# The attention loop of one core issued by whole tiles instead of half tiles, with eight filler products at the start

## The chip, the cores and the metric

The kernel runs on one core of a Trainium2 chip. A core has five instruction streams that run beside each other and wait for one another through semaphores: TensorE (PE, products and transposes; its weight loads are shown as PEld), VectorE (DVE), ScalarE (ACT), GpSimd (POOL) and SyncE (SP), which here only starts DMA transfers. Each stream keeps its own order: an instruction that waits holds up all that stand behind it on its engine. The metric is the device time of one execution in microseconds (us), as the median of several runs.

## The reference

Attention over 2 batches, 8 heads, 768 positions and head size 64, with a band of 96 local keys and 8 global ones, feeds a mixture of 4 experts and then a gated layer:

```python
scores = scale * np.matmul(q, k.transpose(0, 1, 3, 2))
...
scores = np.where(keep, scores + bias, -1000000000.0)
a = np.exp(scores - np.max(scores, axis=-1, keepdims=True))
a = a / (np.sum(a, axis=-1, keepdims=True) + 1e-09)
x = np.matmul(a, v)
...
out += p[:, e:e + 1] * (np.maximum(x @ w1[e], 0.0) @ w2[e])
...
y = ((out @ w1) * (out @ w2) @ w3) @ w_out
```

All is float32. The products behind the attention split each operand into a high and a low part and make three products of one.

## The kernel before

The change touches one function, `banded_attention`, which fills the first 79 us. It works on 12 tiles of 128 queries (6 for each batch). A tile sees 232 keys: 8 global ones, 96 before the tile and its own 128; the first tile of each batch has only its own 128. These two come first in the order of the tiles. The 8 heads of a tile are done in two **steps** of 4 heads, written (tile, 0) and (tile, 1); tiles are counted here in the order in which they are done, so that (1,1) is the second half of the second tile. There are 24 steps.

What a step needs, in the order of its data:

- **S**: 8 score products on PE (L246) into two banks of PSUM, the memory that PE writes and from which DVE and ACT read (tiles `sp`, 4 in turn).
- 4 reductions on DVE (L257), each of which adds the bias of a head and finds its row maximum, then 4 exponentials on ACT (L264), which write `pt` and the row sums. DVE and ACT hand over through the buffers `t`, of which there are 3.
- the inverse of the sums: POOL adds 1e-9 (L230), DVE takes the reciprocal (L232).
- the normalisation of `pt`: heads 0 to 2 on POOL (L304), head 3 on DVE (L308).
- **T**: 8 transposes on PE (L280) into two banks (`tp`, 2 in turn), which I call its half 0 and half 1 (two heads each); DVE copies half 0 (L292) and ACT half 1 (L290) to `ptT`.
- **V**: 16 value products on PE (L322 and L323; only 8, at L325, for the first tile of a batch) into one bank (`op`, 2 in turn).
- the split of the result: ACT writes the high part `xh` from `op` (L391), DVE subtracts it from `op` and writes the low part `xl` (L397).

The engines follow the order in which the code is written (`manual_schedule`). PE goes round by steps: S of step s, T of step s-2, V of step s-3. Steps 11 to 22 also carry one piece each of the split of the experts' first weights: ACT writes the high part (L50) and POOL the low part (L51). At the very start PE runs 11 products on zeros (`keep_warm(WARM)`, L175), and 4, 4 and 2 more behind the scores of steps 0, 1 and 2. At the end, three products of the experts (`up_ahead`, L56 to L58) are put between the last steps. From the first of them the rest of the program is unchanged.

Of the kernel before, what the change touches and what calls it, by code (L numbers as in the profile page):

```python
# [8 lines left out]
F32 = mybir.dt.float32  # L9
# [4 lines left out]
ALU = mybir.AluOpType  # L14
AF = mybir.ActivationFunctionType
# [3 lines left out]
P = 128  # L19
B, H, S, D = 2, 8, 768, 64  # L20
NQ = S // P
# [96 lines left out]
def banded_attention(tc, g, x_hi, x_lo, slots, experts):  # L118
    nc = tc.nc
    with ExitStack() as ctx:  # L120
# [15 lines left out]

        order = [b * NQ for b in range(B)] + [u for u in range(B * NQ) if u % NQ]

        steps = [(u, gr) for u in order for gr in range(2)]

        def place(u):

            return u + 1 if u < NQ else u - NQ
# [80 lines left out]
        raws = []  # L224

        def inverse_sums(u, gr, part):
            hs = slice(4 * gr, 4 * gr + 4)
# [3 lines left out]
            else:  # L231
                nc.vector.reciprocal(r, r)  # L232

        def scores(u, gr, before):
# [16 lines left out]
            sums = st[u]["sums"]  # L251
            pt = two.tile([P, 4, WIN], F32, name="pt", bufs=3)
            for hh in range(4):
                h = 4 * gr + hh
                t = three_.tile([P, WIN], F32, name="t", bufs=3)
                bb = bias[:, h] if i else bias0[:, h]
                nc.vector.tensor_tensor_reduce(  # L257
                    out=t[:, 0:w], in0=sp[hh % 2][:, hh // 2, 0:w], in1=bb, scale=-SCALE,
                    scalar=3.0e38, op0=ALU.add, op1=ALU.min, accum_out=g.negmax[:, u * H + h : u * H + h + 1],
                )  # L260

                if before and hh in (0, 2):
                    inverse_sums(*before, hh // 2)
                nc.scalar.activation(  # L264
                    pt[:, hh, 0:w], t[:, 0:w], AF.Exp, bias=g.negmax[:, u * H + h : u * H + h + 1],
                    scale=-1.0, accum_out=sums[:, h : h + 1],
                )
            st[u][gr] = pt

        def transposes(u, gr):  # L270
            i = u % NQ
            nj = 2 if i else 1
            pt = st[u][gr]
            tps = []
            for half in range(2):
                tp = ps_t.tile([P, 2, 2, P], F32, name="tp")
                for hh in range(2):
                    for j in range(nj):
# [5 lines left out]
        def copies(u, gr):  # L284
            nj = 2 if u % NQ else 1
            res = []
            for half, tp in enumerate(st[u][gr]):
                sb = two.tile([P, 2, 2, P], F32, name="ptT", bufs=4)
                if half:
                    nc.scalar.copy(sb[:, :, 0:nj], tp[:, :, 0:nj])  # L290
                else:
                    nc.vector.tensor_copy(sb[:, :, 0:nj], tp[:, :, 0:nj])  # L292
                res.append(sb)
            st[u][gr] = res

        def normalize(u, gr):
# [13 lines left out]
        def values(u, gr):  # L310

            i = u % NQ
            va, vo = values_of[u]
            o = ps_o.tile([P, 2, 2 * P], F32, name="op")
            st[u].setdefault("o", []).append(o)
            for hh in range(4):
                h, ab = 4 * gr + hh, hh % 2
                sb = st[u][gr][hh // 2]
                os_ = o[ab * D : (ab + 1) * D, hh // 2, 0:P]
                vs = slice(h * D, (h + 1) * D)  # L320
                if i:
                    nc.tensor.matmul(os_, va[:, vs], sb[0 : LW + GW, ab, 0], start=True, stop=False)  # L322
# [2 lines left out]
                    nc.tensor.matmul(os_, vo[:, vs], sb[:, ab, 0], start=True, stop=True)  # L325

        def outputs(u, gr):
            return st[u]["o"][gr][:, :, 0:P], x_hi, x_lo, u, slice(2 * gr, 2 * gr + 2)


        ns = len(steps)
        for s in range(ns + 3):
            n = s - W_STEP
            if 0 <= n <= 12 and n % 4 == 0:
                raws.append(two.tile([P, F], F32, name="wr"))
                nc.sync.dma_start(raws[-1], g.w_moe[0, n // 4])
            if 4 <= s < ns:
                split_x_hi(nc, *outputs(*steps[s - 4]))
            if s < ns:
                u, gr = steps[s]  # L340
                if gr == 0 and s // 2 + 2 < len(order):
                    fetch(order[s // 2 + 2])
                if gr == 1 and s // 2 + 1 < len(order):
                    fetch_v(order[s // 2 + 1])
                scores(u, gr, steps[s - 1] if s else None)
                if s == 0:
                    first_bias(1)
                    later_distances()
                if s in (2, 3):
                    later_bias(s - 2)  # L350
                if s < len(FILL) and FILL[s]:
                    keep_warm(FILL[s])
            if 0 <= s - 2 < ns:
                transposes(*steps[s - 2])
                copies(*steps[s - 2])
            if s == ns:
                inverse_sums(*steps[-1], 0)
                inverse_sums(*steps[-1], 1)
            if 0 <= s - 1 < ns:
                normalize(*steps[s - 1])  # L360
            if 4 <= s < ns:
                split_x_lo(nc, *outputs(*steps[s - 4]))
            if s >= 3:
                values(*steps[s - 3])
            if s >= ns:
                for step in steps[s - 4 : s - 2] if s == ns else (steps[s - 3],):
                    split_x_hi(nc, *outputs(*step))
                for step in steps[s - 4 : s - 2] if s == ns else (steps[s - 3],):
                    split_x_lo(nc, *outputs(*step))
                experts.up_ahead(ps_s)  # L370
            if 2 <= n <= 13:
                f, part = divmod(n - 2, 4)
                ps = slice(part * (F // 4), (part + 1) * (F // 4))
                hi, lo = slots[f]
                split(nc, hi[:, ps], lo[:, ps], raws[f][:, ps], nc.gpsimd)
            if s == ns + 1:
                split(nc, *slots[3], raws[3])


def put_x(nc, g, pool, xn, x_hi, x_lo, u):  # L380
# [865 lines left out]
```

## Time and profile before

| what | value |
|---|---|
| median of 3 runs | 832.16 us (832.11 to 832.34) |
| the profiled execution's own time | 833.32 us |
| its span, first to last instruction | 831.5 us |
| PE busy in the span | 820.7 us, 99% |
| DVE, ACT, POOL busy | 62%, 34%, 37% |
| attention loop | from the start to 79.07 us |

The span is what the trace covers; the execution's own time is longer by what lies around it (1.8 us). Busy shares are means over stages that differ: in the attention loop DVE and ACT are busy nearly all the time, behind it hardly. PE is pipelined, so the distance from the start of one group to the start of the next says more than the duration shown.

### The profile page before, as it was taken

Reading aid. Unit: us, or ns where it says so; the run is one execution under the profiler, and the core shown is the slowest. Engines: PE = TensorE matmul, PEld = TensorE weight load, DVE = VectorE, ACT = ScalarE, POOL = GpSimd, SP = SyncE. Lnnn points to the kernel's source line nnn. Section 1 sums busy time; section 2 is a strip of 40 time slices with the busy share of each in tenths; the row PEclk is TensorE's granted clock in tenths of the full one; section 3 lists DMA queues with packets and bytes.
Section 4 is the critical chain, followed back from the end, with each engine's and each line's share of the span. In section 5 each row is a group of like instructions: output and inputs, shape, how many; then the busy total and the mean of one; then the engine's idle time right before and its main releaser. Section 6 shows DMA issues by size and latency. Waiting matters only on the chain.

```text
span 831.5 us, 11122 instructions
## 1 busy us (share of the span) xinstructions
PE 820.7 (99%) x4006; PEld 668.9 (80%) x4006; DVE 514.9 (62%) x961; ACT 286.5 (34%) x609; POOL 307.7 (37%) x317
## 2 busy tenths in 40 slices
PE   8999999999999999999999999999999999999996
PEld 4777888888888888888888888888788888888875
DVE  7997356557755556787738563665633743887840
ACT  6997321224311213334323321332443332333210
POOL 3686023535356464550344341422380003333300
PEclk9999999999999999999999999999999999999999
DMA  6662233547553556643101101120522210201011
GB/s 205 215 190 64 78 123 106 165 159 238 160 165 114 166 165 202 222 157 103 62 26 52 39 25 64 43 73 27 192 99 91 86 51 26 101 26 51 2 51 55
DMA packets 38295, 88.14 MB, mean 106 GB/s; under 512 B 3722, under 2 KB 10170, under 8 KB 38230
## 3 DMA queue, kind: packets, MB, share of 16 engines
q1 hardware_dynamic: 38230, 87.33, 32.6%
q8 instruction: 34, 0.56, 0.3%
q14 instruction: 31, 0.25, 0.1%
HBM read 73.66 MB, written 13.66 MB: 105 GB/s over the span
## 4 chain that ended last, share of the span: by engine, by line
PE 91%; POOL 3%; ACT 2%; DVE 1%; issue 1%; POOLq 0%; ACTq 0%; DVEq 0%
PE z L56 18%; PE z L58 18%; PE z L57 18%; PE o L58 11%; PE o L56 11%; PE o L57 11%; POOL pt L304 2%; ACT pt L264 1%; POOL sl L51 1%; PE tp L175 1%; PE sp L246 1%; PE tp L280 1%; PE op L322 1%; PE sp L56 0%; PE op L323 0%
## 5 line engine op out<-in xcount | busy, mean ns | idle before, releaser
L58 PE MATMUL z<-xh,sl 128*128 128x512 f32 x428 | 166.6, 389 | 0.0
L56 PE MATMUL z<-xh,sh 128*128 128x512 f32 x428 | 166.5, 389 | 0.0
L57 PE MATMUL z<-xl,sh 128*128 128x512 f32 x428 | 166.5, 389 | 0.0
L494 POOL TENSOR_TENSOR cr<-cr,cb 128x512 f32<-128x512 f32 x40 | 51.6, 1289 | 126.9 <-issue 119.1
L51 POOL TENSOR_TENSOR sl<-wr,sh 128x256 fp32r<-128x256 f32 (+1 forms) x44 | 40.9, 944 | 150.1 <-ACT sh L50 149.5
L58 PEld LDWEIGHTS z<-xh,sl 128*128 128x128 f32 x428 | 80.4, 188 | 17.2 <-DVE sl L51 0.2
L57 PEld LDWEIGHTS z<-xl,sh 128*128 128x128 f32 x428 | 80.4, 188 | 16.8
L56 PEld LDWEIGHTS z<-xh,sh 128*128 128x128 f32 x428 | 80.3, 188 | 16.3
L51 DVE TENSOR_TENSOR sl<-wr,sh 128x1024 fp32r<-128x1024 f32 (+1 forms) x57 | 70.5, 1243 | 23.1 <-ACT sh L50 22.4
L50 ACT CAST sh<-wr 128x1024 fp32r<-128x1024 f32 (+2 forms) x101 | 75.5, 767 | 21.2 <-PE z L57 10.3
L746 POOL TENSOR_TENSOR acc<-acc,t 128x512 f32<-128x512 f32 x36 | 49.3, 1404 | 84.5 <-DVE t L745 84.5
L479 POOL TENSOR_SCALAR ca<-ca 128x512 f32<-128x512 f32 x40 | 61.9, 1548 | 35.3 <-ACT ca L477 35.3
L645 DVE TENSOR_TENSOR t<-t,z 128x512 f32<-128x512 f32 x56 | 37.5, 680 | 32.0 <-PE z L58 27.7
L56 PE MATMUL z<-sh,sh 128*128 128x512 f32 x128 | 49.9, 390 | 0.7 <-DVE t L745 0.7
L58 PE MATMUL z<-sh,sl 128*128 128x512 f32 x128 | 49.8, 389 | 0.0
L57 PE MATMUL z<-sl,sh 128*128 128x512 f32 x128 | 49.8, 389 | 0.0
L264 ACT ACTIVATE pt<-t,negmax 128x232 f32<-128x232 f32 (+1 forms) x96 | 44.3, 462 | 8.7 <-DVE negmax L257 7.6
L304 POOL TENSOR_TENSOR pt<-pt,r 128x232 f32<-128x232 f32 (+1 forms) x72 | 38.0, 555 | 15.5 <-DVE r L232 15.5
L257 DVE CUSTOM_DVE_ANT_0 t<-sp,bias 128x232 f32<-128x232 f32 (+1 forms) x96 | 32.5, 372 | 3.9 <-PE sp L246 3.0
L51 POOL TENSOR_TENSOR sl<-t,sh 128x256 fp32r<-128x256 f32 (+1 forms) x24 | 23.0, 973 | 31.2 <-ACT sh L50 31.0
L56 PE MATMUL o<-h0h,sh 128*128 128x512 f32 x84 | 32.8, 390 | 0.0
L57 PE MATMUL o<-h0l,sh 128*128 128x512 f32 x84 | 32.7, 389 | 0.0
(252 smaller groups left out, 1737.0 us busy)
## 6 DMA issues: line engine op xcount, KB each, us to landing
wr<-in_w_moe_dram SPq DMA_DIRECT2D x44, 512.0 KB
raw<-in_w3t_dram SPq DMA_DIRECT2D x16, 512.0 KB
raw<-in_w_ab_dram SPq DMA_DIRECT2D x16, 512.0 KB
wr<-wab_d SPq DMA_DIRECT2D x16, 512.0 KB
raw<-in_w_out_dram SPq DMA_DIRECT2D x8, 512.0 KB
w3t_d<-cr SPq DMA_DIRECT2D x16, 256.0 KB
wab_d<-cr SPq DMA_DIRECT2D x16, 256.0 KB
wr<-w3t_d SPq DMA_DIRECT2D x8, 512.0 KB
```

Of the source, the lines that this page charges most:

```text
L50: nc.scalar.copy(hi, src)
L51: (lo_engine or nc.vector).tensor_tensor(lo, src, hi.bitcast(F32), op=ALU.subtract)
L56: nc.tensor.matmul(out, wh, xh, start=start, stop=False)
L57: nc.tensor.matmul(out, wh, xl, start=False, stop=False)
L58: nc.tensor.matmul(out, wl, xh, start=False, stop=stop)
L257: nc.vector.tensor_tensor_reduce(out=t[:, 0:w], in0=sp[hh % 2][:, hh // 2, 0:w], in1=bb, scale=-SCALE, scalar=3.0e38, op0=ALU.add, op1=ALU ...
L264: nc.scalar.activation(pt[:, hh, 0:w], t[:, 0:w], AF.Exp, bias=g.negmax[:, u * H + h : u * H + h + 1], scale=-1.0, accum_out=sums[:, h : h ...
L304: nc.gpsimd.tensor_tensor(pt[:, hh, 0:w], pt[:, hh, 0:w], r[:, hh : hh + 1].to_broadcast([P, w]), op=ALU.mult)
L479: nc.gpsimd.tensor_scalar(a, a, 2.0**-15, None, op0=ALU.max)
L494: nc.gpsimd.tensor_tensor(rest, rest, top.bitcast(F32), op=ALU.add)
L645: add = lambda o, a, b: nc.vector.tensor_tensor(o, a, b, op=ALU.add)
L746: nc.gpsimd.tensor_tensor(acc[c][:, d], acc[c][:, d], t, op=ALU.add)
```

## The change

The loop no longer goes round by steps but by tiles. In tile m, with `one_back` and `two_back` for the tiles before, PE now issues S(m,0), S(m,1), T(one_back,0), V(two_back,1), V(one_back,0), T(one_back,1). The other engines' code is written in an order to go with it. Besides that:

- `WARM` is 8 instead of 11.
- V of two steps that follow each other on PE now fills two halves of one bank: `op` is a tile of 4x128 and each step takes 2x128 of it. There are still 2 such banks, and 8 banks in all.
- POOL normalises all 4 heads in the first tiles (m up to 5); from m = 6 on (`shared`) head 3 is DVE's as before.
- `pt` has 4 buffers instead of 3.
- The low parts of two steps (`low(gone)`) follow the copy of T(one_back,0), half 0, on DVE; the high parts (`high(gone)`) end the tile on ACT.

In the changed file the scores are at L244, the reductions at L259, the reciprocal at L230, the transposes at L275, the copies at L282, DVE's normalisation at L297, the values at L314, L315 and L317, and `xl` at L454.

```diff
-WARM = 11
+WARM = 8
...
-            o = ps_o.tile([P, 2, 2 * P], F32, name="op")
-            st[u].setdefault("o", []).append(o)
+            if not banks or len(banks[-1][1]) == 2:
+                banks.append((ps_o.tile([P, 4, P], F32, name="op"), []))
+            o = banks[-1][0][:, 2 * len(banks[-1][1]) :][:, 0:2]
+            banks[-1][1].append((u, gr))
+            st[u]["o", gr] = o
...
-                if hh < 3:
+                if hh < 3 or not shared:
...
-        for s in range(ns + 3):
...
-                scores(u, gr, steps[s - 1] if s else None)
...
-                transposes(*steps[s - 2])
-                copies(*steps[s - 2])
...
-                normalize(*steps[s - 1])
...
-                split_x_lo(nc, *outputs(*steps[s - 4]))
-            if s >= 3:
-                values(*steps[s - 3])
...
+        for m, u in enumerate(order):
+            one_back, two_back = (order[m - k] if m >= k else None for k in (1, 2))
+            shared = 11 <= 2 * m <= 22
...
+            scores(u, 0)
...
+            scores(u, 1)
...
+            if m >= 2:
+                for half in range(2):
+                    copy(two_back, 1, half)
+            rest = piece(2 * m)
+            if m:
+                inverse_sums(one_back, 1, 0)
+            weights(u, 0, 0)
+            if m:
+                inverse_sums(one_back, 1, 1)
+            weights(u, 0, 1)
+            if m:
+                transposes(one_back, 0)
+                copy(one_back, 0, 1)
+            weights(u, 0, 2)
+            weights(u, 0, 3)
...
+            if m:
+                copy(one_back, 0, 0)
+                low(gone)
+                normalize(one_back, 1, shared)
+            rest()
...
+            inverse_sums(u, 0, 0)
+            weights(u, 1, 0)
+            weights(u, 1, 1)
+            inverse_sums(u, 0, 1)
+            weights(u, 1, 2)
+            weights(u, 1, 3)
...
+            normalize(u, 0, shared)
+            rest()
+            gone = [(two_back, 1)] if m >= 2 else []
+            gone += [(one_back, 0)] if m else []
+            for step in gone:
+                values(*step)
+            if m:
+                transposes(one_back, 1)
+            high(gone)
...
+        values(prior, 1)
+        experts.up_ahead(ps_s)
+        values(last, 0)
+        transposes(last, 1)
...
+        experts.up_ahead(ps_s)
+        values(last, 1)
...
+        experts.up_ahead(ps_s)
```

Here a function `weights` is one head's reduction and exponential, `copy` one of the two copies behind a T, `inverse_sums(..., 0)` POOL's part of the inverse and `inverse_sums(..., 1)` DVE's; `rest` is a weight piece's low part on POOL.

The order of the instructions on two engines shows the move. The number behind a name is the program's number of that buffer's use (an `op` with the same number is the same bank in the same use), and what an instruction waits for is given as the engine or DMA queue whose semaphore it watches.

PE before, one step in the middle of the loop (`sp` scores, `tp` transposes, `op` values):

```order
L246 MATMUL sp_925<-keys_96,qr_638 128x232
...
L280 MATMUL tp_946<-ident_63,pt_818 128x128 [waits DVE_49,Pool_49]
...
L280 MATMUL tp_951<-ident_63,pt_818 128x128 [waits Activation_49,Pool_49]
...
L322 MATMUL op_965<-ptT_900,va_695 64x128 [waits DMAHW7_49,DVE_49]
L323 MATMUL op_965<-ptT_900,vo_693 64x128 [waits DMAHW6_49]
...
L322 MATMUL op_965<-ptT_902,va_695 64x128
...
L246 MATMUL sp_980<-keys_96,qr_749 128x232 [waits DMAHW1_49,DMAHW0_49]
```

One S, one T and one V alternate, and each V has a bank of its own number.

PE after, tile m = 7 from the end of its scores on:

```order
L244 MATMUL sp_867<-keys_96,qr_627 128x232 [waits DVE_49]
...
L275 MATMUL tp_887<-ident_63,pt_754 128x128 [waits DVE_49,Pool_49]
...
L275 MATMUL tp_892<-ident_63,pt_754 128x128 [waits Activation_49,Pool_49]
...
L314 MATMUL op_830<-ptT_874,va_524 64x128 [waits DVE_49]
...
L314 MATMUL op_830<-ptT_876,va_524 64x128
...
L314 MATMUL op_942<-ptT_905,va_632 64x128 [waits DMAHW7_49]
...
L314 MATMUL op_942<-ptT_897,va_632 64x128 [waits Activation_49]
...
L275 MATMUL tp_951<-ident_63,pt_761 128x128 [waits PE_49,Pool_49]
```

The first V (`op_830`, the second half of a bank whose first half the tile before has filled) stands right behind T(one_back,0) and waits for DVE; the second V (`op_942`, a new bank) reads `ptT_905`, which DVE writes, and has no wait for DVE of its own.

DVE before, around one copy (`xl` is the low part, `r` the sums):

```order
L257 ISA t_943,negmax_69<-sp_926,bias_97 128x232 [waits Activation_49]
...
L292 COPY ptT_956<-tp_946 128x512 [waits PE_49]
L308 TENSOR_SCALAR pt_875<-pt_875,r_874 128x232 [waits DVE_49]
L397 TENSOR_TENSOR xl1_74<-op_909,xh1_71 128x2x128
L257 ISA t_989,negmax_69<-sp_980,bias_97 128x232 [waits PE_49,Activation_49]
```

The low part there reads `op_909`, while PE is at `op_965`, another bank.

DVE after, in tile m = 7, from the copy of T(two_back,1) to the normalisation:

```order
L282 COPY ptT_874<-tp_839 128x512 [waits PE_49]
L259 ISA t_880,negmax_69<-sp_858,bias_97 128x232 [waits PE_49,Activation_49]
...
L230 RECIPROCAL r_753<-r_753 128x4 [waits Pool_49]
L259 ISA t_884,negmax_69<-sp_859,bias_97 128x232 [waits PE_49,Activation_49]
...
L282 COPY ptT_905<-tp_887 128x512 [waits PE_49]
L454 TENSOR_TENSOR xl0_73<-op_716,xh0_70 128x2x128
L454 TENSOR_TENSOR xl1_74<-op_830,xh1_71 128x2x128
L297 TENSOR_SCALAR pt_761<-pt_761,r_753 128x232 [waits DVE_49]
```

Two low parts now follow each other behind the copy of `tp_887`, and the second reads `op_830`, the bank whose other half PE's first V of this tile writes.

## Rows read from the trace of the kernel before

**Rows 1.** The page: busy time of each engine, its share, and instructions.

```profile
PE 820.7 (99%) x4006; PEld 668.9 (80%) x4006; DVE 514.9 (62%) x961; ACT 286.5 (34%) x609; POOL 307.7 (37%) x317
```

**Rows 2.** Windows: busy us (instructions) of PE, PEld, DVE, ACT, POOL; clock, DMA, GB/s.

```profile
10.00:20.00 10.00, 8.53 (x72) 5.06 (x69) 9.35 (x54) 9.97 (x44) 5.57 (x16) 1.00 0.63 192
26.00:38.00 12.00, 12.00 (x127) 9.46 (x124) 11.00 (x47) 10.49 (x39) 7.15 (x16) 1.00 0.64 203
41.00:72.00 31.00, 31.00 (x322) 24.21 (x320) 28.70 (x122) 30.31 (x111) 26.13 (x51) 1.00 0.57 176
```

**Rows 3.** Timeline of PE, one step: start, duration, engine, line, tiles, shapes, count.

```profile
29.38 1.05 PE L246 MATMUL sp<-keys,qr 64*128 64x232 f32 x8
30.37 1.09 PE L280 MATMUL tp<-ident,pt 128*128 128x128 f32 x8
31.39 0.45 PE L322 MATMUL op<-ptT,va 104*64 104x128 f32 x4
31.66 0.40 PE L323 MATMUL op<-ptT,vo 128*64 128x128 f32 x4
31.88 0.44 PE L322 MATMUL op<-ptT,va 104*64 104x128 f32 x4
...
32.47 0.47 PE L246 MATMUL sp<-keys,qr 64*128 64x232 f32 x2
```

**Rows 4.** Chain of waits in order of time, one later step: start, duration, work.

```profile
44.01 0.23 POOL r L230
44.26 0.19 DVE r L232
...
44.59 1.67 POOL pt L304 x3
46.31 0.73 POOL sl L51
...
47.11 0.23 POOL r L230
```

**Rows 5.** Timeline of DVE over the step of rows 3.

```profile
30.58 0.40 DVE L257 CUSTOM_DVE_ANT_0 t<-sp,bias 128x232 f32<-128x232 f32 x1 [0.23 <-PE sp L246]
...
31.54 0.17 DVE L232 RECIPROCAL r<-r 128x4 f32<-128x4 f32 x1
31.69 0.40 DVE L257 CUSTOM_DVE_ANT_0 t<-sp,bias 128x232 f32<-128x232 f32 x1
...
32.02 0.69 DVE L292 COPY ptT<-tp 128x512 f32<-128x512 f32 x1
32.62 0.48 DVE L308 TENSOR_SCALAR pt<-pt,r 128x232 f32<-128x232 f32 x1
33.03 0.41 DVE L397 TENSOR_TENSOR xl<-op,xh 128x256 fp32r<-128x256 f32 x1
```

**Rows 6.** Timeline of PE at the start.

```profile
1.17 4.87 PE L175 MATMUL tp<-warm 128*128 128x512 bf16 x11 [1.17 <-DVE warm L169]
5.97 1.10 PE L246 MATMUL sp<-keys,qr 64*128 64x128 f32 x8
7.01 1.04 PE L175 MATMUL tp<-warm 128*128 128x512 bf16 x4
```

**Rows 7.** Timeline of all engines, 16 to 23 us.

```profile
16.77 0.49 ACT L264 ACTIVATE pt<-t,negmax 128x232 f32<-128x232 f32 x1
...
18.20 0.47 ACT L264 ACTIVATE pt<-t,negmax 128x232 f32<-128x232 f32 x1
...
18.86 0.22 POOL L230 TENSOR_SCALAR r<-sums 128x4 f32<-128x4 f32 x1 [0.18 <-ACT pt L264]
...
22.37 0.66 PE L325 MATMUL op<-ptT,vo 128*64 128x128 f32 x8
```

**Rows 8.** Timeline of PE at the end of the loop.

```profile
71.78 0.45 PE L322 MATMUL op<-ptT,va 104*64 104x128 f32 x4
...
79.07 0.50 PE L56 MATMUL sp<-xh,sh 128*128 128x512 f32 x1
```

More of the change, by code (lines that the diff above doesn't have):

```diff
@@ L250, in scores, with weights @@
                 )
[L251 to L268, printed above, removed]
+            st[u]["sp", gr] = sp
+            st[u][gr] = two.tile([P, 4, WIN], F32, name="pt", bufs=4)
+        def weights(u, gr, hh):
+            w = WIN if u % NQ else P
+            h = 4 * gr + hh
+            t = three_.tile([P, WIN], F32, name="t", bufs=3)
+            bb = bias[:, h] if u % NQ else bias0[:, h]
+            nm = g.negmax[:, u * H + h : u * H + h + 1]
+            nc.vector.tensor_tensor_reduce(
+                out=t[:, 0:w], in0=st[u]["sp", gr][hh % 2][:, hh // 2, 0:w], in1=bb, scale=-SCALE,
+                scalar=3.0e38, op0=ALU.add, op1=ALU.min, accum_out=nm,
+            )
+            nc.scalar.activation(
+                st[u][gr][:, hh, 0:w], t[:, 0:w], AF.Exp, bias=nm, scale=-1.0, accum_out=st[u]["sums"][:, h : h + 1]
+            )
         def transposes(u, gr):
-            i = u % NQ
-            nj = 2 if i else 1
             pt = st[u][gr]
@@ L277, in transposes @@
                 for hh in range(2):
-                    for j in range(nj):
+                    for j in range(2 if u % NQ else 1):
                         c = slice(j * (LW + GW), j * (LW + GW) + P)
@@ L282, in transposes, with copy, normalize @@
             st[u][gr] = tps
-        def copies(u, gr):
+        def copy(u, gr, half):
             nj = 2 if u % NQ else 1
[L286 to L296, printed above, removed]
+            sb = two.tile([P, 2, 2, P], F32, name="ptT", bufs=4)
+            (nc.scalar.copy if half else nc.vector.tensor_copy)(sb[:, :, 0:nj], st[u][gr][half][:, :, 0:nj])
+            st[u][gr][half] = sb
+        def normalize(u, gr, shared):
             w = WIN if u % NQ else P
@@ L371, in banded_attention, with piece @@
[L371 to L377, printed above, removed]
+        def piece(s):
+            n = s - W_STEP
+            if not 2 <= n <= 13:
+                return lambda: None
+            f, part = divmod(n - 2, 4)
+            ps = slice(part * (F // 4), (part + 1) * (F // 4))
+            hi, lo = (t[:, ps] for t in slots[f])
+            raw = raws[f][:, ps]
+            nc.scalar.copy(hi, raw)
+            return lambda: nc.gpsimd.tensor_tensor(lo, raw, hi.bitcast(F32), op=ALU.subtract)
@@ new lines, in high, with low @@
+        def high(steps):
+            for step in steps:
+                split_x_hi(nc, *outputs(*step))
+        def low(steps):
+            for step in steps:
+                split_x_lo(nc, *outputs(*step))
+        nt = len(order)
+        for m, u in enumerate(order):
+            one_back, two_back = (order[m - k] if m >= k else None for k in (1, 2))
+            shared = 11 <= 2 * m <= 22
+            load_weight(2 * m)
+            load_weight(2 * m + 1)
+            if m + 2 < nt:
+                fetch(order[m + 2])
+            if m + 1 < nt:
+                fetch_v(order[m + 1])
+            scores(u, 0)
+            if m == 0:
+                keep_warm(FILL[0])
+            scores(u, 1)
+            if m < 2:
+                keep_warm(FILL[m + 1])
+            if m >= 2:
[13 more added lines that the diff above has]
+            weights(u, 0, 3)
+            if m == 0:
+                first_bias(1)
+            if m:
[3 more added lines that the diff above has]
+            rest()
+            if m == 1:
+                later_bias(0)
+            rest = piece(2 * m + 1)
+            inverse_sums(u, 0, 0)
[4 more added lines that the diff above has]
+            weights(u, 1, 3)
+            if m == 0:
+                later_distances()
+            if m == 1:
+                later_bias(1)
+            normalize(u, 0, shared)
[7 more added lines that the diff above has]
+            high(gone)
@@ new lines, in banded_attention @@
+        last, prior = order[-1], order[-2]
+        inverse_sums(last, 1, 0)
+        for half in range(2):
+            copy(prior, 1, half)
+        inverse_sums(last, 1, 1)
+        transposes(last, 0)
+        low(gone)
+        normalize(last, 1, True)
+        for half in range(2):
+            copy(last, 0, half)
+        values(prior, 1)
+        experts.up_ahead(ps_s)
+        values(last, 0)
+        transposes(last, 1)
+        for half in range(2):
+            copy(last, 1, half)
+        high([(prior, 1), (last, 0)])
```

42 lines of the change are left out of this document (9 added, 33 removed).

## The prediction

> **What bounds the kernel now.** I read the page first. PE is busy for 820.7 of the 831.5 us [rows 1], so all but 11 us of the kernel is PE's own work: a change can win little unless it removes products or idle time of PE, and loses whatever it makes PE wait. The only products removed are three fillers. Then I read the attention loop by windows. Between 26 and 38 us PE is busy for all of 12.00 us; between 41 and 72 for all of 31.00, with ACT at 30.31 and DVE at 28.70; between 10 and 20 PE has gaps (8.53 of 10) and ACT is nearly full (9.97). The granted clock is 1.00, the 2.4 GHz level, in all three [rows 2]. A busy PE here is not a PE at its peak, so I took the loop's pace from two other views. In PE's timeline a step is S at 29.38, T at 30.37, V at 31.39 and the next S at 32.47: 0.99 + 1.02 + 1.08 = 3.09 us [rows 3]. In the later stretch the chain of waits goes round on POOL: sums at 44.01, reciprocal on DVE at 44.26, three heads normalised from 44.59 (1.67), a weight piece (0.73), the next sums at 47.11: 3.10 us a step [rows 4]. So PE and POOL both go round in 3.1 us a step, or 6.2 a tile, and two engines must both stay free of waits for the loop to get no longer. Over the loop, from V(1,1) at 22.37 [rows 7] to V(9,1) at 71.78 [rows 8], 16 steps take 49.41 us, 3.09 each.
>
> **The wait that the change adds.** After, two V share a bank. In tile m the first V (call it V', of (two_back,1)) writes the second half of a bank of which the first half was filled a tile earlier, and that half's low part is read by the second `xl` of this same tile. The order rows show it from both sides. On DVE the second `xl` reads `op_830`, which is V''s bank. On PE, V' waits for DVE; the V behind it reads `ptT_905`, which DVE's copy writes, and needs no further wait for DVE. So V''s wait must already reach to that copy or behind it, although V' itself reads only `ptT_874`, copied much earlier. Behind the copy stand the two `xl`, and the second is the one with V''s bank. The copy in turn needs T(one_back,0), which PE issues immediately ahead of V'. PE therefore starts a T, waits for DVE to copy its half and to make two `xl`, and only then goes on. Nothing else on PE can fill this: V, T and the next tile's S are queued behind V'.
>
> Before, a V also waits for an `xl`, but one of a bank used two steps earlier, long done; PE's window without a gap says that it costs nothing [rows 2].
>
> By the Trainium skill, page "PSUM — Partial Sum Buffer", section Terms, TensorE writing a bank while VectorE accesses the same bank and quadrant is an error, so this wait could not be dropped by looking at halves of columns. No run here shows such an error; by that page the sum below stands as it is, and a V' that waits only for its copies would not exist.
>
> **A tile after, as a ring.** From V' to the next V', through DVE:
>
> - V' and V on PE: 1.08 for the first, and for the second 0.88, four pairs at the pitch of 0.22 within a group (31.66 to 31.88) [rows 3]: 1.96.
> - T(one_back,1): 1.02 [rows 3].
> - the next S(m,0) to the first reduction on DVE: 29.38 [rows 3] to 30.58 [rows 5]: 1.20.
> - that reduction: 0.32, a third of the three from 30.58 to 31.54. Then the reciprocal, 0.15 (31.54 to 31.69), and three reductions: 0.32 + 0.32 + 0.33 (the last one from 31.69 to 32.02). Together 1.44 until the copy starts [rows 5].
> - the copy to what follows it: 0.60 (32.02 to 32.62) [rows 5].
> - two `xl`: 0.41 each [rows 5], of which the second overlaps the first by 0.08 as one reduction does the other (0.40 long, 0.32 apart): 0.74.
> - handing over to PE: an estimate of 0.07, between the 0.02 (44.24 to 44.26) and 0.14 (44.45 to 44.59) that POOL and DVE take to hand over to each other [rows 4].
>
> Sum: 1.96 + 1.02 + 1.20 + 1.44 + 0.60 + 0.74 + 0.07 = **7.03 us a tile**. The copy must also have its transposes. PE comes to T(one_back,0) after two S, 1.98, and its first half takes some 0.55 to 0.7 with the way to DVE: the copy could start 2.5 to 2.7 after S(m,0), against 2.64 by DVE's own chain. The two paths are nearly even, which gives 6.90 to 7.10, and one late reduction or another instruction slipped in brings 7.3. I take 7.03, with 6.9 and 7.3 as bounds. Zero is excluded as a lower bound, since the copy cannot start before T. PE's own work in a tile is 2 x (0.99 + 1.02) + 1.96 = 5.98, so PE idles for 1.05 of it, ahead of V'. POOL, DVE and ACT do in a tile what they did in two steps (26.13, 28.70 and 30.31 of 31 us for ten steps [rows 2]), and all fit into 7.03 (ACT the tightest: 6.06).
>
> **The sum.** Three parts, each against before.
>
> 1. *Opening, to V'(3), which is V(1,1).* Eleven fillers take 4.87 us, 0.443 each; three fewer let the first S start 1.28 to 1.33 us earlier than 5.97, at about 4.7. The next fillers run at 0.26 each [rows 6]. How much of this lead reaches the third tile is not shown: ACT is the full engine there [rows 2], and it can begin earlier by at most that. I take about 1.0 of it, so that the third tile's first exponential (16.77 before) starts at 15.8; bounds 15.5 and 17. From here V'(3) hangs on step (2,0): its four exponentials take 1.43 (16.77 to 18.20) plus 0.3 for a copy that now stands between them on ACT: 17.53. The sums follow 0.66 later (18.20 to 18.86) [rows 7]: 18.19; the normalisation 0.58 after that (44.01 to 44.59): 18.77; four heads on POOL instead of three, 4 x 0.55 from the 1.67 for three [rows 4]: 20.97. POOL's sums for (2,1) stand behind that, and DVE's reciprocal behind them: 0.07 + 0.25 = 21.29. The three reductions and the reciprocal's pitch to the copy are 1.1, the copy and two `xl` and the handing over 0.60 + 0.74 + 0.07: V'(3) at 23.8 against 22.37 [rows 7]: **+1.4** (bounds +1.1 to +2.7).
> 2. *Eight rounds, V'(3) to V'(11).* 8 x 7.03 less 0.4, since the first V' belongs to a first tile and has 8 products instead of 16 (0.66 [rows 7] against 1.08): 55.8 against 49.41: **+6.4** (bounds +5.4 to +8.6).
> 3. *Tail, V'(11) to the first product of the experts.* After, two V (1.96) with the last T between and a third step's copies: 1.96 + 1.02 + some 1.4 until the last transposes are copied and a bank is free + 1.08 = 5.5. Before: 71.78 to 79.07, 7.29 [rows 8]. **-1.8** (bounds -2.5 to -1.0), since more of the loop's work is done by then.
>
> Sum: +1.4 + 6.4 - 1.8 = +6.0. The rest of the program is PE without gaps and moves by as much. The profiled execution took 833.32, so its like after is 839.3, with the first experts' product at about 85.1; it lies 1.16 above the median of 832.16, and the median should follow at **838.2 us**. What costs nothing: the fourth `pt` buffer and POOL's fourth head (2 x (0.58 + 4 x 0.55) = 5.6 of 7.03 in tiles that carry no weight pieces [rows 4]). DMA starts by tiles rather than by steps, under a DMA share of 0.57 to 0.64 [rows 2].
>
> **Rivals.**
>
> - *No wait for the bank, chance 0.09.* If V' needs only its own copies, PE runs on and the next ring decides. From recip(one_back,1) DVE makes three reductions (1.12), the copy (0.60), two `xl` (0.66 at their pitch), head 3 (0.41) and two reductions (0.64) before recip(m,0): 3.43; POOL's leg from there to the next reciprocal is the 3.10 of today [rows 4, 5]. 6.53 in the five rounds with weight pieces, 5.98 in the three before: 50.2 for the eight rounds, +0.8; the opening 0.4 later by POOL's fourth head and the tail 1.0 shorter (estimates): 832.4, no change. For it: only the order stands behind the wait. Against it: V has no wait for DVE of its own, which only a wait of V' that far along explains. It turns to this if V' starts within 0.2 us of the end of T(one_back,0).
> - *Faster, chance 0.04.* The same, and recip(m,0) does not stand behind the copy's work, so that POOL's ring stays at 6.20 a tile: 3 x 5.98 + 5 x 6.20 - 0.4 = 48.5, -0.9, with the same -0.6 from opening and tail 830.7, and under 830.5 if the opening keeps its whole lead of 1.28. It needs both links to be absent and that lead.
> - *Much slower, chance 0.03.* PE's waits of 1.05 us in every tile make the clock fall to the 1.2 GHz level; PE's 5.98 would double part of the time, some +4 us a tile, 865 or more. Against it: between 10 and 20 us PE idles 1.47 of 10 at a granted clock of 1.00 [rows 2], about the share expected here (1.05 of 7.03).
> - *Bank wait with sizes off, 0.84 in all.* 836.5 to 840.5 for the most part; a late DVE in every tile (7.3 or more) gives 840.5 to 842, chance 0.04; 834 to 836.5 if the opening keeps all its lead and the tail is short, chance 0.04.
>
> **How the numbers follow.** The bank wait is the likeliest (0.84), and its sum is the forecast. Its bounds for the parts do not all fall on one side, so its own range is 836.5 to 840.5; I widen to 835.8 and 840.8. Left out are the 0.13 of the cases without it, about 0.03 of the clock, and little of the sizes: 2 in 10. A measurement of this kernel tells 0.2%, 1.66 us, from no change: 830.5 to 833.8. The case without the wait and a hundredth of the bank's give same 0.10; faster is 0.04, slower the remaining 0.86.
>
> **What the changed profile would show.** The first V of a tile (L314) with about 1.05 us idle ahead of it, released by DVE's `xl` at L454; PE busy 84 to 86% between 30 and 70 us instead of 100%; tiles 7.0 us apart; S at 4.7; the first experts' product (L56) at about 85. If PE shows no gap there, the bank argument is wrong; if the gap is there but the tile takes other than 7.03, the DVE chain from S to the copy is mis-sized; if the opening's V'(3) is not at about 23.8, the exponentials' start is.

## The result, and the profile after

| | before | after | ratio |
|---|---|---|---|
| median, 6 runs each | 832.35 us (832.11 to 833.18) | 840.08 us (839.3 to 840.79) | 1.0090 [1.0077, 1.0103] |
| profiled execution, its span | 833.32, 831.5 | 840.34, 838.0 | |
| first product of the experts starts | 79.07 [rows 8] | 85.50 | |

The change makes the kernel 0.9% slower. Three of its six executions have a mean granted clock of 0.999 and took 839.30 to 839.97 us; the other three, the profiled one among them, have 0.996 or 0.997 and took 840.18 to 840.79.

The page's busy line, to be held against [rows 1]: PE is busy for 5.1 us less, and the span is 6.5 us longer.

```profile
PE 815.6 (97%) x4002; PEld 670.0 (80%) x4003; DVE 509.2 (61%) x950; ACT 287.9 (34%) x609; POOL 312.7 (37%) x328
```

The windows, in the stretches of [rows 2] (busy us and instructions of PE, PEld, DVE, ACT and POOL, then granted clock, DMA share, GB/s):

```profile
10.00:20.00 10.00, 7.46 (x62) 5.39 (x62) 7.96 (x45) 9.84 (x43) 7.13 (x20) 0.92 0.64 185
26.00:38.00 12.00, 9.64 (x100) 8.05 (x99) 8.66 (x38) 9.72 (x36) 8.66 (x18) 1.00 0.69 213
41.00:72.00 31.00, 26.02 (x280) 21.94 (x278) 23.95 (x107) 27.04 (x95) 23.14 (x46) 1.00 0.60 189
```

PE had no gap between 26 and 72 us before; now it is busy for 9.64 of 12 and 26.02 of 31. No other engine is fuller for it: between 41 and 72 us DVE, ACT and POOL all do less. So no engine has become the bottleneck; each of them waits somewhere. PE's timeline shows where (start, duration, line, tiles, shapes, count; in brackets the idle time ahead and who ended it):

```profile
44.80 0.45 PE L314 MATMUL op<-ptT,va 104*64 104x128 f32 x4 [1.18 <-DVE xl L454]
...
46.76 1.09 PE L275 MATMUL tp<-ident,pt 128*128 128x128 f32 x8
47.78 1.84 PE L244 MATMUL sp<-keys,qr 64*128 64x232 f32 x16
49.55 1.09 PE L275 MATMUL tp<-ident,pt 128*128 128x128 f32 x8
51.82 0.45 PE L314 MATMUL op<-ptT,va 104*64 104x128 f32 x4 [1.18 <-DVE xl L454]
```

The first value product of a tile (V', L314) has 1.18 us of idle PE ahead of it, ended by `xl` on DVE, and the tiles are 51.82 - 44.80 = 7.02 us apart. DVE's side of the same tile:

```profile
48.98 0.40 DVE L259 CUSTOM_DVE_ANT_0 t<-sp,bias 128x232 f32<-128x232 f32 x1 [0.83 <-PE sp L244]
...
49.30 0.17 DVE L230 RECIPROCAL r<-r 128x4 f32<-128x4 f32 x1
...
50.42 0.69 DVE L282 COPY ptT<-tp 128x512 f32<-128x512 f32 x1
51.02 0.75 DVE L454 TENSOR_TENSOR xl<-op,xh 128x256 fp32r<-128x256 f32 x2
```

The first reduction waits for the scores (0.83), then come the reciprocal, the copy at 50.42 and the two `xl` at 51.02, 0.75 for both; V' starts at 51.82. This closes a ring: V' waits for the second `xl`, and DVE's chain to it starts with scores that PE makes only behind the V' of the tile before. Over the loop the view of PE's waits adds this one up (us in total, times, longest):

```profile
PE op L314 <- DVE xl L454: 9.4, 8, 1.2
```

At the end of the loop, V'(11) and the experts' first product:

```profile
79.92 0.45 PE L314 MATMUL op<-ptT,va 104*64 104x128 f32 x4 [1.18 <-DVE xl L454]
...
85.50 0.51 PE L56 MATMUL sp<-xh,sh 128*128 128x512 f32 x1
```

### The profile page after: what moved, and what is told of

Same layout as the page of the kernel before. It is cut to its first block, busy times and chain, and to the rows that moved or that the text cites. A ratio compares the mean times of both kernels' runs of the same rounds, so it can differ in the third digit from the quotient of the medians.

```text
span 838.0 us, 11056 instructions
## 1 busy us (share of the span) xinstructions
PE 815.6 (97%) x4002; PEld 670.0 (80%) x4003; DVE 509.2 (61%) x950; ACT 287.9 (34%) x609; POOL 312.7 (37%) x328
## 4 chain that ended last, share of the span: by engine, by line
PE 93%; DVE 4%; ACT 1%; issue 1%; POOL 0%; DVEq 0%; ACTq 0%
PE z L56 18%; PE z L57 18%; PE z L58 18%; PE o L56 11%; PE o L58 11%; PE o L57 11%; PE tp L275 1%; PE sp L244 1%; PE op L314 1%; DVE t L259 1%; PE op L315 1%; DVE ptT L282 1%; DVE xl L454 1%; ACT pt L263 1%; PE tp L173 0%
## 5 line engine op out<-in xcount | busy, mean ns | idle before, releaser
L51 POOL TENSOR_TENSOR sl<-wr,sh 128x512 fp32r<-128x512 f32 (+1 forms) x32 | 32.1, 1024 | 149.5 <-ACT sh L50 149.5
L50 ACT CAST sh<-wr 128x1024 fp32r<-128x1024 f32 (+2 forms) x89 | 70.6, 816 | 21.4 <-PE z L57 10.3
L293 POOL TENSOR_TENSOR pt<-pt,r 128x232 f32<-128x232 f32 (+1 forms) x83 | 43.6, 555 | 14.2 <-DVE r L230 12.2
L259 DVE CUSTOM_DVE_ANT_0 t<-sp,bias 128x232 f32<-128x232 f32 (+1 forms) x96 | 33.5, 371 | 10.0 <-PE sp L244 8.7
```

The lines of the kernel that those rows point to most:

```text
L50: nc.scalar.copy(hi, src)
L51: (lo_engine or nc.vector).tensor_tensor(lo, src, hi.bitcast(F32), op=ALU.subtract)
L259: nc.vector.tensor_tensor_reduce(out=t[:, 0:w], in0=st[u]["sp", gr][hh % 2][:, hh // 2, 0:w], in1=bb, scale=-SCALE, scalar=3.0e38, op0=ALU ...
L293: nc.gpsimd.tensor_tensor(pt[:, hh, 0:w], pt[:, hh, 0:w], r[:, hh : hh + 1].to_broadcast([P, w]), op=ALU.mult)
```

## The experiments

Each ran beside the kernel before on the same chip (whose median there was 832.93 to 833.25 us); ratios are to that. The change itself stands at 1.0090. An interval that holds 1 shows no difference.

| kernel | median us | ratio |
|---|---|---|
| one bank for the two V of a tile | 834.11 | 1.0017 [1.0008, 1.0026] |
| low parts early | 832.53 | 0.9995 [0.9986, 1.0004] |
| low parts swapped | 836.60 | 1.0041 [1.0028, 1.0054] |
| a bank for each V | 837.52 | 1.0053 [1.0039, 1.0068] |
| before, with shared banks | 867.21 | 1.0401 [1.0380, 1.0422] |
| change, 11 fillers | 840.94 | 1.0099 [1.0083, 1.0114] |
| before, 8 fillers | 832.83 | 1.0005 [0.9996, 1.0014] |
| low parts early, one bank a tile | 834.12 | 1.0016 [1.0007, 1.0025] |
| low parts early, a bank for each V | 832.38 | 0.9991 [0.9982, 1.0000] |
| low parts early, one bank a tile, experts' first product early | 833.67 | 1.0007 [0.9998, 1.0016] |
| low parts early, tail laid out anew | 832.02 | 0.9987 [0.9978, 0.9996] |
| low parts early, tail laid out anew, head 3 always on DVE | 831.38 | 0.9982 [0.9973, 0.9991] |

**One bank for the two V of a tile.** Nothing moves on any engine; only which two V share a bank changes.

```diff
-            if not banks or len(banks[-1][1]) == 2:
+            if not banks or gr == 1:
```

> The two value groups that fill one bank are (two_back,1) and (one_back,0) of the same tile, instead of (one_back,0) and the (two_back,1) of the next tile; nothing moves on any engine. Bank theory: the first value group has only its copies to wait for, the gap of 1.18 us ahead of it goes, a tile takes 6.0 to 6.1 us without weight pieces and 6.2 to 6.5 with them, and the median falls from 840 to 831.5 to 833. Rival (the length of VectorE's chain from the scores to the second low part sets the pace, whichever bank is used): the gap stays, 7.0 us a tile, 840.

PE's timeline, from V(1,1) to the experts:

```profile
21.04 0.66 PE L317 MATMUL op<-ptT,vo 128*64 128x128 f32 x8
...
27.54 0.45 PE L314 MATMUL op<-ptT,va 104*64 104x128 f32 x4
...
33.34 0.45 PE L314 MATMUL op<-ptT,va 104*64 104x128 f32 x4
...
52.49 0.45 PE L314 MATMUL op<-ptT,va 104*64 104x128 f32 x4
...
53.87 0.45 PE L314 MATMUL op<-ptT,va 104*64 104x128 f32 x4 [0.24 <-DVE ptT L282]
...
58.95 0.45 PE L314 MATMUL op<-ptT,va 104*64 104x128 f32 x4
...
71.90 0.45 PE L314 MATMUL op<-ptT,va 104*64 104x128 f32 x4
...
76.69 0.63 PE L275 MATMUL tp<-ident,pt 128*128 128x128 f32 x4 [1.23 <-DVE ptT L282]
...
79.45 0.50 PE L56 MATMUL sp<-xh,sh 128*128 128x512 f32 x1
```

No value product waits for `xl` any more. Tiles are 33.34 - 27.54 = 5.80 us apart without weight pieces and 58.95 - 52.49 = 6.46 with them, where the second V waits 0.24 for its copy. V'(3), which is V(1,1), to V'(11) takes 71.90 - 21.04 = 50.86 us against 55.76 in the change. The experts start at 79.45, 6.05 us earlier than in the change: of the 6.43 us that it lost by that place, the choice of the bank alone is 6.05. They are 3.12 in the opening (V(1,1) at 21.04 instead of 24.16; the granted clock fell there in the change's profiled execution and not in this one, so not all of the 3.12 need be waiting), 4.90 in the eight rounds, and 1.97 the other way in the tail. The medians agree: this kernel is 1.02 us above the kernel before beside it, the change 7.73. The length of DVE's chain, which is the same here, is refuted as the cause. The median came out 1.1 us above the range expected, of which 0.7 is the kernel before beside it, at 833.09 instead of 832.35.

**Low parts swapped, and a bank for each V.** Two ways to make V' wait for the first low part instead of the second:

```diff
-                low(gone)
+                low(gone[::-1])
```

```diff
-            if not banks or len(banks[-1][1]) == 2:
-                banks.append((ps_o.tile([P, 4, P], F32, name="op"), []))
-            o = banks[-1][0][:, 2 * len(banks[-1][1]) :][:, 0:2]
-            banks[-1][1].append((u, gr))
+            o = ps_o.tile([P, 4, P], F32, name="op")[:, 0:2]
```

> The two low parts change places: the one that reads the shared bank comes first. Bank theory: TensorE's first value group starts one low part earlier, 0.33 to 0.35 us in each tile, so the tile takes 6.7 us and the median is 837.0 to 837.6. Rival (VectorE's chain length): the chain is as long as before, 7.0 us a tile, 840.

> Each value group has a bank of its own again, 2 in turn, in the new order. Bank theory: that does not take the wait away, since the bank of the first value group is the one that the same group used a tile earlier, and its low part, now the first of the two, still stands behind the copy: 6.7 us a tile, 837.0 to 837.6, as with the low parts swapped. Rival (it is the sharing that costs): the gap goes, 832 to 833.

PE's timeline of the first:

```profile
49.98 0.45 PE L314 MATMUL op<-ptT,va 104*64 104x128 f32 x4 [0.85 <-DVE xl L454]
...
56.67 0.45 PE L314 MATMUL op<-ptT,va 104*64 104x128 f32 x4 [0.85 <-DVE xl L454]
```

and of the second, where the line numbers are 3 lower:

```profile
56.28 0.45 PE L311 MATMUL op<-ptT,va 104*64 104x128 f32 x4 [0.84 <-DVE xl L451]
```

In both the wait is 0.84 to 0.85 instead of 1.18 and a tile takes 6.69 instead of 7.02 (in the second V' starts at 49.59 and 56.28): one `xl`, 0.33 us, in every tile, as the bank theory had it. Undoing the sharing does not take the wait away, since the bank's turn of two still comes round to a low part behind the copy. The medians, 836.60 and 837.52, were both expected at 837.0 to 837.6: the first lies 0.4 below that.

**Low parts early.** They go to where DVE waited for the scores.

```diff
+            if m:
+                low(gone)
             rest = piece(2 * m)
...
                 copy(one_back, 0, 0)
-                low(gone)
```

> The two low parts stand ahead of the tile's first reduction on VectorE, where it was idle for 0.83 us, instead of behind the copy; banks as in the change. Bank theory: the low parts are done before the scores are, the gap goes; VectorE's chain between its two reciprocals is 0.7 us shorter as well, so tiles take 6.0 to 6.1 us, and 6.2 with weight pieces (GpSimd's own work), and the median is 830 to 832. Rival (VectorE's chain length): 0.74 less a tile, 6.3 us, 834.

```profile
28.23 0.45 PE L314 MATMUL op<-ptT,va 104*64 104x128 f32 x4
...
34.07 0.45 PE L314 MATMUL op<-ptT,va 104*64 104x128 f32 x4
...
52.66 0.45 PE L314 MATMUL op<-ptT,va 104*64 104x128 f32 x4
...
58.78 0.45 PE L314 MATMUL op<-ptT,va 104*64 104x128 f32 x4
...
77.80 0.50 PE L56 MATMUL sp<-xh,sh 128*128 128x512 f32 x1
```

PE's timeline shows 34.07 - 28.23 = 5.84 us a tile, and 58.78 - 52.66 = 6.12 with weight pieces. The experts start at 77.80, 1.27 us before the kernel before. The median shows less of it: 832.53, where 830 to 832 was expected, against 833.09 beside it, a ratio of 0.9995 whose interval holds 1. Some 0.5 us of the gain are lost outside the span, where an execution of this kernel spends 2.25 to 2.43 us and one of the kernel before 1.73 to 1.90.

**Before, with shared banks.** The sharing alone, in the order by steps.

```diff
-        raws = []
+        raws, banks = [], []
...
-            o = ps_o.tile([P, 2, 2 * P], F32, name="op")
+            if not banks or len(banks[-1][1]) == 2:
+                banks.append((ps_o.tile([P, 4, P], F32, name="op"), []))
+            o = banks[-1][0][:, 2 * len(banks[-1][1]) :][:, 0:2]
+            banks[-1][1].append((u, gr))
```

> The kernel before, with nothing changed but the banks: two value groups that follow each other share one, as in the change. Bank theory: in the order by steps every second value group must wait for the low part of the group ahead of it, which stands behind the copy and head 3 on VectorE and ends 2.05 us after that value group used to start; two steps take 7.6 to 8.3 us instead of 6.18, the loop 11 to 17 us more, the median 844 to 849. Rival (sharing a bank costs only in the new order): 832 to 833.

```profile
46.20 0.45 PE L325 MATMUL op<-ptT,va 104*64 104x128 f32 x4 [2.03 <-DVE xl L400]
...
47.28 1.76 PE L246 MATMUL sp<-keys,qr 64*128 64x232 f32 x8
48.98 1.97 PE L280 MATMUL tp<-ident,pt 128*128 128x128 f32 x8
...
56.28 0.45 PE L325 MATMUL op<-ptT,va 104*64 104x128 f32 x4 [2.25 <-DVE xl L400]
```

The wait is there in every second step, 2.03 and 2.25 us by PE's timeline, as expected. But two steps take 56.28 - 46.20 = 10.08 us, not 7.6 to 8.3. A window of that stretch says why the price is higher:

```profile
40.00:50.00 10.00, 7.97 (x68) 6.28 (x67) 6.16 (x29) 5.89 (x21) 3.78 (x8) 0.84 0.36 110
```

The granted clock is 0.84 there, where it was 1.00 before [rows 2]. In windows of 1 us it is 1.00 (the 2.4 GHz level) up to 47, 0.74 in the next, 0.50 (the 1.2 GHz level) from 48 to 50, 0.55 in the next and 1.00 again from 51, after PE had been idle from 44.17 to 46.20; the S and T that follow the wait at 46.20 take 3.59 us (47.28 to 50.87) instead of 2.01. The bank theory named the wait and its length; the time that I put on it, 849 at most, was 18 us short of the 867.21, mostly because I priced all that follows the wait at full clock.

**Fillers.**

```diff
-WARM = 8
+WARM = 11
```

in the change, and the reverse in the kernel before.

> The change with eleven filler products at first instead of eight. Lead theory (most of the lead of 1.28 us that three fewer fillers give lasts to the third tile, since ScalarE is full there): the first scores move from 4.70 to 5.97, the value group (1,1) from 24.2 to 25.2, and the median is 0.9 to 1.3 us above that of the change. Rival (the lead is eaten up, or paid back by a granted clock of 0.56 to 0.58 that the change showed between 18 and 22 us): within 0.4 us of the change, with a clock of 1.00 there.

> The kernel before with eight filler products at first, and nothing else. Lead theory: the value group (1,1) starts 0.9 to 1.2 us earlier than 22.37, and the median is 0.8 to 1.2 us below the kernel before. Rival (the opening hangs on transfers or on the bias work on VectorE): no difference beyond 0.3 us.

The change with 11 fillers, PE's timeline:

```profile
5.71 0.71 PE L244 MATMUL sp<-keys,qr 64*128 64x128 f32 x8
...
25.09 0.66 PE L317 MATMUL op<-ptT,vo 128*64 128x128 f32 x8 [1.01 <-DVE xl L454]
```

The lead of 1.01 us at the first scores is 0.93 at V(1,1) (25.09 against 24.16), and the median is 0.86 above that of the change. The lead theory holds in the profile (the experts start at 86.43, 0.93 later); the median is just under its range of 0.9 to 1.3. The granted clock falls with 11 fillers too (0.76 from 18 to 20 us, 0.50 from 20 to 22), so the missing fillers are not what made it fall. The kernel before with 8:

```profile
20.77 0.66 PE L325 MATMUL op<-ptT,vo 128*64 128x128 f32 x8
```

V(1,1) is 1.60 us earlier, but the median is not lower: the expectation missed. Part of the lead is given back later. At the start of the gated layer PE waits for DVE, 0.71 us in the kernel before and here

```profile
595.03 0.47 PE L56 MATMUL z<-sh,sh 128*128 128x512 f32 x1 [1.58 <-DVE t L745]
```

1.58, by 0.87 more. Part of the rest is the clock: five of its eleven executions have a mean granted clock of 0.995 or 0.996 and took 833.89 to 834.61 us, against 4 of 27 of the kernel before beside it. But even the other six have a median of 832.64, against 832.71 for the other 23 of the kernel before; why the lead does not show there I did not find out. In part it may be the one execution that was profiled: kernels with the same opening reach the same V at 17.23 and at 17.75 (the two with both repairs, below).

**Both repairs together**, the early low parts and one bank a tile, and one product of the experts ahead of the last T(11,0) besides:

```diff
+        experts.up_ahead(ps_s)
         transposes(last, 0)
...
         values(prior, 1)
-        experts.up_ahead(ps_s)
```

> Both repairs: the low parts ahead of the tile's first reduction, and one bank for the two value groups of a tile. Bank theory: each of the two takes the whole wait away, so together they give what the early low parts give alone, within 0.4 us. Rival (each removes its own part): a further 0.5 to 1.5 us less.

> Both repairs, and in the tail the first product of the experts stands ahead of the last tile's first transposes, where TensorE was idle for 0.85 and 0.35 us. Theory (TensorE bounds all that follows, so an idle time filled there is won in full): 1.0 to 1.4 us less than both repairs without it. Rival (the copies or the low parts of the last steps are late next): less than 0.5.

Together they are 1.6 us worse than the early low parts alone (0.2% by the ratios, since the two ran on different chips), which neither theory had. The chain of waits shows it. Early low parts with the banks of the change:

```profile
56.89 0.27 ACT xh L449
57.18 0.76 DVE xl L455 x2
```

and with one bank a tile:

```profile
58.20 0.53 ACT xh L449 x2
...
58.76 0.75 DVE xl L455 x2
```

With the two V of a tile in one bank, DVE's first `xl` starts only behind both `xh` of ACT (0.53) instead of the first (0.27), and the tile takes 6.39 instead of 6.13, 0.26 us more. By the Trainium skill, page "PSUM — Partial Sum Buffer", section "PSUM bank collisions raise a hardware error", two engines that only read one bank at the same time collide too. No run here shows such a collision; the order in these traces agrees with it, since DVE's read of the bank starts only when ACT's second read of it has ended.

The early product won 0.45 of the 1.0 to 1.4 expected, which is what the rival had (less than 0.5). PE's gap moved on to the V behind the next, which waits for a copy that on DVE now stands behind the split of that product's result (0.69 us at 80.25), the two `xl` and head 3:

```profile
82.51 0.45 PE L314 MATMUL op<-ptT,va 104*64 104x128 f32 x4 [0.97 <-DVE ptT L282]
```

**A bank for each V, with early low parts.** The test of that reading, with the edit shown above:

> The early low parts, with a bank of its own for each value group. With early low parts and one bank for the groups of a tile the first low part waits for both high parts, since ScalarE and VectorE read one bank in turn, and a tile takes 6.39 us; with early low parts and the banks of the change it waits for one, and the tile takes 6.13. Theory: with banks of their own it waits for one too, 6.13 us a tile, and the median is that of the early low parts alone, 831.5 to 832.7. Rival (the banks of the change are better for another reason): 6.3 to 6.4, 834.

The tile is 6.12 us again (V' at 52.47 and 58.59), and the first `xl` follows one `xh` of 0.27: confirmed. The median, 832.38, lies in the range expected.

**The tail laid out anew, and head 3 always on DVE.**

```diff
         inverse_sums(last, 1, 1)
-        transposes(last, 0)
         low(gone)
         normalize(last, 1, True)
+        experts.up_ahead(ps_s)
+        transposes(last, 0)
...
         values(prior, 1)
+        split(nc, *slots[3], raws[3])
         experts.up_ahead(ps_s)
         values(last, 0)
...
         low([(last, 1)])
-        split(nc, *slots[3], raws[3])
-        experts.up_ahead(ps_s)
```

This is the tail; within the loop, `low(gone)` stands at the start of a tile as in the early low parts. The second kernel has `shared = True` for all tiles besides.

> The early low parts with the banks of the change, and the tail laid out anew: each of the three products of the experts stands one place earlier (ahead of the last tile's first transposes, ahead of its first values, ahead of its last values), low parts and head 3 ahead of the copies, and the last weight split earlier. Theory (what follows is TensorE without gaps, so the idle 0.85 and 0.35 us of the tail are won): 1.0 to 1.4 us less than the early low parts alone, some 0.15% below the kernel before. Rival (a later copy or the weight split takes it back): within 0.4 us of the early low parts.

> As the one before, and VectorE normalises head 3 in all tiles, not only in those with weight pieces. Theory (the opening hangs on GpSimd's normalisation, 0.55 us for a head): the value group (1,1) starts 0.4 to 0.6 us earlier, and the median is that much lower. Rival (the opening is ScalarE's, which is nearly full there): no difference.

The first is at 0.9987, 0.5 us below the early low parts alone (832.53 to 832.02; 0.08% by the ratios) where 1.0 to 1.4 was expected, and the rival had at most 0.4: a gap of 0.92 came up behind the last V, at a product that waits for the last `xl`:

```profile
88.68 0.50 PE L56 MATMUL o<-h0h,sh 128*128 128x512 f32 x1 [0.92 <-DVE xl L455]
```

The second is at 0.9982, the fastest of all and 0.09 to 0.27% faster than the kernel before. Its 0.6 us over the first are in the range expected, but not for the reason expected: in its profiled execution, where the granted clock fell to 0.50 at 18 to 20 us, V(1,1) came at 22.64, against 21.48 in the first. PE's timeline shows where that was won back. In the first kernel a V at 41.43, in the round where GpSimd's first weight pieces fall, waits 0.62 for a copy on DVE, and that round takes 6.67 us (S at 36.87 to S at 43.54); with head 3 on DVE from the start the wait is gone and the round takes 6.12 (37.25 to 43.37). Some 0.2 of the 0.6 us lie outside the span (2.06 to 2.19 us there, against 2.24 to 2.34). What V(1,1) would gain at full clock stays open.

## Why the prediction was right

**The place of the wait** was the one named: the first V of a tile, idle by 1.18 us (1.05 forecast), released by the second `xl`, eight times in the stretch; PE is busy 33.37 of 40 us between 30 and 70, 83% (84 to 86). That it is the bank, and not DVE's chain as such, is shown by the first experiment.

**The ring of 7.03** was 7.02. This is not luck: each link came out as it stood in the sum. From the starts shown above, V' and V take 1.96 (44.80 to 46.76), T 1.02, S to the first reduction 1.20, from there to the copy 1.44, the copy 0.60, and the two `xl` with the handing over 0.80 where I had 0.81. The links were intervals between two starts in the trace of before, not busy times. The other path to the copy, through T, was not as close as I had it: two S in a row take 1.77 (47.78 to 49.55) instead of 1.98, so T was done early, which is also why the wait was 1.18 and not 1.05.

**The sum.** From the starts: V(1,1) at 24.16 instead of 22.37, +1.79 (forecast +1.4); eight rounds 55.76 instead of 49.41, +6.35 (+6.4); tail 85.50 - 79.92 = 5.58 instead of 7.29, -1.71 (-1.8). Together +6.43 at the experts' first product, where I had +6.0.

**The term that was mis-sized** is the opening. Its links up to GpSimd's normalisation came some 0.55 us earlier than I had them, and then more than that was lost again:

```profile
16.98 0.49 ACT L263 ACTIVATE pt<-t,negmax 128x232 f32<-128x232 f32 x1
...
17.64 0.22 POOL L228 TENSOR_SCALAR r<-sums 128x4 f32<-128x4 f32 x1 [1.23 <-ACT pt L263]
...
18.23 2.17 POOL L293 TENSOR_TENSOR pt<-pt,r 128x232 f32<-128x232 f32 x4 [0.37 <-PE op L317]
...
20.95 0.40 DVE L259 CUSTOM_DVE_ANT_0 t<-sp,bias 128x232 f32<-128x232 f32 x1 [1.92 <-PE sp L244]
```

The last exponential of (2,0) started at 16.98 (17.53 forecast), the sums at 17.64 (18.19), the four heads at 18.23. But DVE's next reduction then idled 1.92 us for scores, and PE's timeline and the windows behind it show what kept them:

```profile
17.04 1.09 PE L317 MATMUL op<-ptT,vo 128*64 128x128 f32 x16 [1.09 <-DVE xl L454]
...
18.89 3.23 PE L244 MATMUL sp<-keys,qr 64*128 64x232 f32 x16
...
24.16 0.66 PE L317 MATMUL op<-ptT,vo 128*64 128x128 f32 x8 [1.01 <-DVE xl L454]
```

```profile
16.00:18.00 2.00, 0.96 (x16) 0.85 (x16) 1.72 (x10) 2.00 (x10) 0.64 (x3) 1.00 0.03 8
18.00:20.00 2.00, 2.00 (x14) 1.51 (x12) 1.03 (x6) 2.00 (x10) 1.77 (x4) 0.58 0.63 163
20.00:22.00 2.00, 2.00 (x14) 1.53 (x10) 1.05 (x7) 0.81 (x4) 1.03 (x3) 0.56 0.83 232
22.00:24.00 2.00, 1.15 (x10) 0.86 (x8) 1.72 (x7) 1.32 (x5) 1.77 (x4) 1.00 0.38 117
```

16 score products took 3.23 us there, against 1.84 for 16 in a tile of the loop. PE had waited 1.09 for an `xl` ahead of V at 17.04, and was busy for 0.96 of the 2 us from 16 to 18; from 18 to 22 the granted clock was 0.58 and 0.56, near the 1.2 GHz level, and at 1.00 again from 22 on. I had called a fall of the clock the rival of 0.03 and read the window from 10 to 20 us of before against it. The fall came, for four microseconds of the opening, not in the tiles: those stayed at 1.00 with 1.18 us of idle time in each. What it cost can be estimated. The kernels with both repairs, without and with the experts' product early, have the same opening; in the profiled execution of the first the clock fell to 0.50 there, and V(1,1) started 5.55 us behind the V before it (17.23 to 22.78); in that of the second it stayed at 1.00, and the same way took 4.26 (17.75 to 22.01; 4.25 with the early low parts alone, also at 1.00). That is 1.29 us. The change's executions with a mean clock of 0.999 are 0.7 us shorter by the median than its others. So without the fall the opening would have lost some 0.5 to 1.1 (an estimate from these two): my +1.4 was too high for an opening at full clock, and that it came near the +1.79 of the profiled execution is in part luck.

**The step from the profile to the median** lost more than the sum. I took over that the profiled execution lies 1.16 above the median; after the change it lies 0.26 above. And the time around the span, which I took as fixed, is 2.34 us (840.34 - 838.0) instead of 1.82. The profiled executions differ by 7.02 us, 6.5 of it in the span; the medians by 7.73 over six runs each. So the forecast of 838.2 was 1.9 below the measured 840.08, which lies inside the range of 835.8 to 840.8 but near its upper end.

**The rivals.** With the wait for the bank removed, the next ring was as worked out: 6.46 us a tile with weight pieces (6.53 forecast) and 5.80 without (5.98), at 1.0017 of the kernel before, so "no change" was the right answer to that case. But its sum came out by errors that cancel, which is luck: the opening was 1.33 earlier than before instead of 0.4 later, the eight rounds lost 1.45 instead of 0.8, and the tail, which I had 1.0 shorter, was 0.26 longer: 79.45 - 71.90 = 7.55 against 7.29, since the transposes of the last tile then wait for copies (1.23). I take the change's shorter tail for slack that its slow rounds had given to ACT and DVE; no run shows that by itself.

## What to carry to other kernels

When two groups of products share a bank, look at which reader of the first group's half stands where on its own engine: the second group waits for that reader, and for all that is queued ahead of it. Here it stood behind a copy that needs the very transposes issued just ahead of the waiting group, so PE could not run ahead and the wait came back in every round; choosing the other partner for the bank, or moving the reader to where its engine was idle, each took it away. And two repairs of one wait need not add: together they made a new wait, of DVE for ACT's second read. With the wait gone, the new order gained at most 0.27% on the old: PE was busy for 99% of the span before.

## What the runs showed of the hardware that was not expected

- The granted clock fell to 0.58 and 0.56 for about 4 us at the start of the loop in the profiled execution of the change, and to 0.50 or 0.51 there in those with the low parts swapped, with both repairs, with 11 fillers and in the fastest version. It stayed at 1.00 there with one bank a tile, a bank for each V and early low parts alone. What PE did just before does not tell the two apart: with both repairs, without and with the experts' product early, it waited 0.87 us for the same copy and was busy for 1.13 of the 2 us from 16 to 18, and from 18 to 20 the clock was 0.50 in the one and 1.00 in the other. No run tells what does. In the tiles of the change, 1.18 us of idle time in 7.02 left it at 1.00; in the kernel before with shared banks, 2.03 and 2.25 us in 10.08 went with 0.84.
- The time around the span depends on the program: 1.73 to 1.91 us in all runs of the kernel before, 2.27 to 2.38 in those of the change, 1.97 to 2.15 with one bank a tile or a bank for each V. No run tells why.
